# Two warming products, a fourth pair of banks for the first turns, modelled places for rectified differences, copies on VectorE, and a whole-row projection with single weighings in the last unit

## The chip, the cores and the metric

The kernel runs on one NeuronCore of one Trainium2 chip. The metric is the device time of one execution in microseconds. TensorE (PE, with its weight loads shown as PEld), VectorE (DVE), ScalarE (ACT), GpSimd (POOL) and SyncE (SP, which issues nearly all DMAs) run their own instruction streams in order and wait for each other by semaphores.

## The reference

One transformer block on a sequence of S = 2048 tokens of width D = 640: attention with H = 32 heads of 20, then a gated feed-forward of width F = 1728, both on layer-normed input and both added to it. All is float32.

```python
qkv = layernorm(x) @ wqkv                      # split into q, k, v and heads
scores = q @ k.T * Dh ** -0.5                  # per head
p = softmax(scores, axis=-1)
h = x + (p @ v) @ wo
z = layernorm(h)
h2 = h + (silu(z @ w_gate) * (z @ w_up)) @ w_down
```

## The kernel before

Products with full precision are made of three: each operand is split into a rounded high part and the rest (`split`: ACT copies, another engine subtracts), and hi·hi, hi·lo and lo·hi are summed in one PSUM bank. There are eight banks of 128 x 512.

**Beginning.** `load_x(0)` brings four tiles of 128 tokens. While they land, `warm` runs products that nothing reads (`ident` by the last of these tiles, L898), on a pair of banks from `ps_wide`. `norm(0)` normalises the tiles on DVE (L755); `flip_tokens` turns each by five TensorE transposes into a pair of banks (L801) and splits it from there into z_hi (ACT, L96) and z_lo (DVE, L97). `ps_wide` hands out its pairs of banks in rotation (`wide_places`). `first_blocks` then makes the first block of queries and the first block of keys (L826) in two banks with fixed numbers.

**Projection stage, to about 334 us.** A list `work` of blocks (`query_key`: 128 rows of queries or keys for 512 tokens) and values (`value`) runs in order. Their products (L569) use 64 rows of the array each, one half of the array beside the other. Between them stand turns of the next tokens (`flip`, L783), and products that find the maximum of each row of scores beforehand, as softmax needs it. These come in two kinds: pairs (L194), where the difference of two key blocks gives max(a, b) as relu(b − a) + a, with both parts of 256 columns in one bank; and opened products (L217), where a first product is rectified by ACT (L231) into a *place* in SBUF, and a second product, issued later on the same half, is added to it and maximised by DVE (L224). There are three such places, `relus`, taken in rotation by `next_place`. A key block or query block for these products is brought back from DRAM (`stack`, L161) into a free tile; tiles that are borrowed get the constant rows that they need by copying a piece of `w_hi` (`raw_place`, then `place`, L379, on ACT, four copies of 128 x 1024).

What order all this stands in is decided while the program is written, by a planner. The class `Halves` holds modelled clocks for the two halves, for each engine and for each bank; `use(engine, us)` advances one; `pair`, `finish_second`, `flip`, `run` and `keep` place the next instruction where these clocks say that nothing waits. The lengths in it (0.5 us for a copy of a block by ACT, for instance) are numbers in the code. On the chip the engines run this order with real semaphores: where a modelled length is too short, the engine waits, and all behind it on that engine. `self.second` holds the opened product of each half, at most one. `queries_at` says when the loaded queries of a unit are taken to have landed.

**Attention, units 0 to 31, to about 1476 us.** A unit is 4 heads by 512 queries. It has 16 steps over key tiles: four score products (`scores`, L1374, 62 rows, one half of the array each), their exponentials on ACT (L1380), and one `weigh` (L1384, four products of 32 columns on all 128 rows). `ORDER` is a string of the operations of a step; with no maxima left it is `sSsSW`. The letter W also runs one entry of `extra`: in the last unit (31) eight projections of the output by `wo` for chunk 1 (`projection`, L1103), three of layer norm, an empty one, and four turns (`flip`, L1135), one per step. With `halved` a projection is thirty products of 64 rows on the two halves, in two banks, added up by two DVE additions (L1109); without, it is fifteen of 128 rows in one bank. In the last unit `both` makes W run two weighings in each even step and none in odd ones.

**Feed-forward, to the end.** The same units of weights pass through rings of buffers; nothing here is touched.

Of the kernel before, what the change touches and what calls it, by code (L numbers as in the profile page):

```python
# [24 lines left out]
NT = S // P  # L25
# [15 lines left out]
MARGIN = 0.2  # L41
BEHIND = 2
# [7 lines left out]
def tile_block(ctx: ExitStack, tc: tile.TileContext, x, wqkv, wo, wg, wu, wd, out):  # L50
# [22 lines left out]
    wide_places, one_places = [2, 4, 6], []  # L73
# [264 lines left out]
    with tc.tile_pool(name="pa", bufs=2) as pa:  # L338
# [33 lines left out]
        def raw_place():  # L372
            return place(raw_tile().rearrange("p a b -> p (a b)")[:, : 2 * CH], nc.scalar)

        def place(t, engine=nc.sync):

            if engine is nc.scalar:
                some = w_hi.rearrange("p k c -> p (k c)")[:, : 2 * CH].bitcast(F32)
                nc.scalar.activation(t, some, AF.Copy)  # L379
# [64 lines left out]
        def staged_keys(u, kc, ks, q=None, since=0):  # L444
# [9 lines left out]
            def one(t, pair, b, at):  # L454
                rows = queries[u] if q is None else items[q][3]
                if b is None:
                    max_differences(mxs[u], rows, items[ks[0]][3], pair, t, kc, next_place(), at)
                    return over()
                first, more = (items[k][3] for k in ks)
                second = max_twice(mxs[u], rows, first, more, pair, t, kc, b, next_place(), at)  # L460
                return lambda at: (second(at), over())
# [15 lines left out]
            if u == 0:  # L477
# [5 lines left out]
                    lambda at, a=a: one(*a, at), a[2],  # L483
# [34 lines left out]
        def next_place():  # L518
            relus.append(relus.pop(0))
            return relus[-1]  # L520
# [9 lines left out]
        class Halves:  # L530
# [74 lines left out]
            def pair(self):  # L605
# [11 lines left out]
                if half is None and any(self.second) or half is not None and self.second[half]:  # L617
                    return False
# [3 lines left out]
                second = queue.pop(ahead)[1](at)  # L622
                if half is not None:
# [3 lines left out]
                    self.second[half] = second, seen  # L627
# [43 lines left out]
            def finish_second(self, half):  # L671
                if not self.second[half]:
                    return False
                second, seen = self.second[half]
# [3 lines left out]
                self.second[half] = None  # L678
                second(at)
                start = self.stream(half, 0.231)  # L680
                self.places[at[0]] = self.use("vector", 0.62, max(seen, start + 0.43)) + 0.14
                return True
# [136 lines left out]
        def first_blocks():  # L819

            z_hi, z_lo = zs[0]
            pss = ps_at(range(2))
# [7 lines left out]
            for m, ps in enumerate(pss):  # L830
                pe.places[m] = keep(0, m, ps)

        def keep(c, m, ps):
# [63 lines left out]
        for _ in range(3):  # L897
# [34 lines left out]
        for at, (kind, c, *which) in enumerate(work):  # L932
# [522 lines left out]
    for u in range(NU):  # L1455
# [4 lines left out]
        for kt in range(NT):  # L1460
# [5 lines left out]
            for op in order:  # L1466
# [4 lines left out]
                else:  # L1471
                    both = u == NU - 1 and kt < NT - 1
# [617 lines left out]
```

## Time and profile before

| | us |
|---|---|
| median of three runs (lowest, highest) | 2037.76 (2036.97, 2040.04) |
| the profiled execution, its own time | 2040.81 |
| its span, from first to last instruction | 2039.0 |
| granted TensorE clock, mean over the span | 0.996 |
| PE busy in the span | 2009.1 |
| ACT, DVE, POOL busy in the span | 1463.3, 1616.7, 778.5 |

Rows of a timeline read: start in us from the span's start, length in us, engine, line, operation, output and input tiles with shapes, count; in brackets the idle time of the engine before it and what ended it. The length of a row of several instructions is from the first start to the last end, and products overlap: from one to the next is shorter than one product's own length. `64*128` or `62*128` behind a product are the rows and columns of the array that it uses. Tiles have the names of the buffers that they borrow: queries and places appear as q_stk or v_stk, key blocks as k_stk or raw.

### The profile page before, as it was taken

Reading aid. Unit: us, or ns where it says so; the run is one execution under the profiler, and the core shown is the slowest. Engines: PE = TensorE matmul, PEld = TensorE weight load, DVE = VectorE, ACT = ScalarE, POOL = GpSimd, SP = SyncE. Lnnn points to the kernel's source line nnn. Section 1 sums busy time; section 2 is a strip of 40 time slices with the busy share of each in tenths; the row PEclk is TensorE's granted clock in tenths of the full one; section 3 lists DMA queues with packets and bytes.
Section 4 is the critical chain, followed back from the end, with each engine's and each line's share of the span. In section 5 each row is a group of like instructions: output and inputs, shape, how many; then the busy total and the mean of one; then the engine's idle time right before and its main releaser. Section 6 shows DMA issues by size and latency. Waiting matters only on the chain.

```text
span 2039.0 us, 39356 instructions
## 1 busy us (share of the span) xinstructions
PE 2009.1 (99%) x13836; PEld 1244.3 (61%) x13836; DVE 1616.7 (79%) x3261; ACT 1463.3 (72%) x2948; POOL 778.5 (38%) x1075
## 2 busy tenths in 40 slices
PE   7999999999999999999999999999999999999998
PEld 6888897333333333333333333345598888888888
DVE  7769776888888888888888888886478666676677
ACT  4887887999999999999999999996634222212221
POOL 4464342234343434344430011001146454754555
PEclk9999999999999999999999999999999999999999
DMA  7775574343533534444433123211159654974642
GB/s 228 236 214 184 167 215 116 104 137 103 150 125 108 158 112 143 135 145 137 149 127 108 30 61 83 82 62 49 36 180 325 208 193 154 350 267 158 204 149 92
DMA packets 205206, 304.93 MB, mean 150 GB/s; under 512 B 47648, under 2 KB 82720, under 8 KB 203984
## 3 DMA queue, kind: packets, MB, share of 16 engines
q1 hardware_dynamic: 204912, 302.40, 45.6%
q8 instruction: 110, 1.80, 0.4%
q14 instruction: 88, 0.72, 0.1%
q10 hardware_dynamic: 96, 0.00, 0.0%
HBM read 205.78 MB, written 95.68 MB: 148 GB/s over the span
## 4 chain that ended last, share of the span: by engine, by line
PE 94%; DMA 2%; DVE 1%; ACT 1%; POOL 1%; issue 1%; SPq 0%; DVEq 0%; ACTq 0%; POOLq 0%
PE banks L1384 25%; PE banks L1374 17%; PE banks L1552 16%; PE banks L238 12%; PE banks L1646 8%; PE banks L569 8%; PE banks L1103 3%; PE banks L217 3%; PE banks L194 1%; DMA qk_d<-e 0%; PE banks L826 0%; PE banks L263 0%; DMA q_stk<-qk_d 0%; ACT q_stk L231 0%; DMA xt<-in_A_x 0%
## 5 line engine op out<-in xcount | busy, mean ns | idle before, releaser
L1380 ACT ACTIVATE probs<-banks 128x512 f32<-128x512 f32 x2048 | 1056.2, 614 | 61.1 <-PE banks L1374 25.3
L244 DVE TENSOR_REDUCE mx<-banks 128x1 f32<-128x512 f32 x1472 | 925.4, 684 | 124.9 <-PE banks L238 76.3
L1374 PE MATMUL banks<-q_stk,k_stk 62*128 62x512 f32 x2048 | 583.2, 428 | 1.5 <-ACT probs L1380 1.5
L1384 PE MATMUL banks<-probs,v_stk 128*32 128x512 f32 x4096 | 545.4, 606 | 0.0
L238 PE MATMUL banks<-k_stk,q_stk 60*128 60x512 f32 x1472 | 486.7, 438 | 0.2
L1374 PEld LDWEIGHTS banks<-q_stk,k_stk 62*128 62x128 f32 x2048 | 291.8, 184 | 283.7 <-ACT probs L1380 271.4
L238 PEld LDWEIGHTS banks<-k_stk,q_stk 60*128 60x128 f32 x1472 | 244.2, 184 | 163.1 <-DVE mx L244 126.8
L1769 DVE TENSOR_TENSOR tmp<-banks,tmp 128x512 f32<-128x512 f32 x208 | 141.2, 689 | 118.4 <-PE banks L1552 92.8
L1384 PEld LDWEIGHTS banks<-probs,v_stk 128*32 128x32 f32 x4096 | 81.3, 108 | 183.1 <-issue 171.4
L1646 PE MATMUL banks<-halves,yp 128*128 128x320 f32 x1032 | 178.9, 308 | 1.4 <-POOL yp L97 1.2
L1646 PEld LDWEIGHTS banks<-halves,yp 128*128 128x128 f32 x1032 | 165.2, 188 | 17.4 <-POOL yp L97 1.5
L1552 PE MATMUL banks<-t,units 128*128 128x512 f32 x624 | 162.7, 396 | 0.1
L97 POOL TENSOR_TENSOR yp<-y,yp 128x256 fp32r<-128x256 f32 x96 | 60.3, 628 | 195.2 <-ACT yp L96 181.0
L1552 PE MATMUL banks<-z,units 128*128 128x512 f32 x516 | 133.8, 394 | 0.0
L255 POOL CAST both<-neg 128x16 fp32r<-128x16 f32 x32 | 6.6, 206 | 314.7 <-PE banks L1374 138.2
L1552 PEld LDWEIGHTS banks<-t,units 128*128 128x128 f32 x624 | 112.5, 188 | 18.9 <-DVE tmp L1769 0.3
L1651 DVE TENSOR_TENSOR h<-banks,h 128x320 f32<-128x320 f32 x248 | 110.0, 481 | 6.8 <-PE banks L1646 5.4
L224 DVE CUSTOM_DVE_ANT_0 q_stk<-banks,q_stk 128x512 f32<-128x512 f32 x139 | 92.7, 687 | 26.0 <-PE banks L217 13.2
L569 PE MATMUL banks<-z_hi,w_hi 64*128 64x512 f32 x380 | 102.4, 406 | 1.9 <-ACT z_hi L96 1.8
L569 PE MATMUL banks<-z_lo,w_hi 64*128 64x512 f32 x380 | 103.3, 395 | 0.0
L1552 PEld LDWEIGHTS banks<-z,units 128*128 128x128 f32 x516 | 93.1, 187 | 16.1 <-DVE tmp L1769 0.2
L96 ACT ACTIVATE yp<-tmp 128x512 fp32r<-128x512 f32 x40 | 25.3, 632 | 103.2 <-POOL tmp L1639 103.2
(213 smaller groups left out, 2960.9 us busy)
## 6 DMA issues: line engine op xcount, KB each, us to landing
units<-w_d SPq DMA_DIRECT2D x186, 256.0 KB
w_d<-stage SPq DMA_DIRECT2D x106, 256.0 KB
halves<-j_d SPq DMA_DIRECT2D x70, 320.0 KB
k_stk<-qk_d SPq DMA_DIRECT2D x116, 160.0 KB
j_d<-stage SPq DMA_DIRECT2D x42, 320.0 KB
q_stk<-qk_d SPq DMA_DIRECT2D x64, 160.0 KB
k_stk<-qk_d SPq DMA_DIRECT2D x116, 80.0 KB
rb<-r_d SPq DMA_DIRECT2D x32, 256.0 KB
```

Of the source, the lines that this page charges most:

```text
L217: nc.tensor.matmul(ps, q[rows, pair, t * P : (t + 1) * P], k[rows, pair, :], start=True, stop=True)
L224: nc.vector.tensor_tensor_reduce(out=place, in0=ps, in1=place, scale=1.0, scalar=LEAST, op0=ALU.add, op1=ALU.max, accum_out=mx[:, b, pair, ...
L238: nc.tensor.matmul(ps, queries[u][rows, pair, t * P : (t + 1) * P], keys[u // NC][rows, pair, kc * CH : (kc + 1) * CH], start=True, stop=True,
L244: nc.vector.tensor_reduce(mxs[u][:, b, pair, t, kc : kc + 1], ps, axis=AX.X, op=ALU.max)
L569: product = nc.tensor.matmul(job["ps"][:, :out], lhs, rhs, start=(half == 0 and i == 0), stop=(half == 1 and i == job["n"] - 1),)
L1374: nc.tensor.matmul(ps, keys[u // NC][rows, p, kt * P : (kt + 1) * P], queries[u][rows, p, :], start=True, stop=True,)
L1380: nc.scalar.activation(probs[p][:, b, :], ps, AF.Exp, scale=scale)
L1384: nc.tensor.matmul(acc[32 * j : 32 * j + 32, :], values[u // NC][:, kt, j * VW : j * VW + 32], probs[j // 2][:, j % 2, :], start=(kt == 0) ...
L1552: nc.tensor.matmul(ps.rearrange("p (t n) -> p t n", t=TPC), w[k][:, i], z[k][:, :, j], start=(first and m == 0), stop=(last and m == len(n ...
L1646: nc.tensor.matmul(ps, a, b, start=(n == 0), stop=(n == len(pairs) - 1))
L1651: nc.vector.tensor_tensor(out=h, in0=ps, in1=h, op=ALU.add)
L1769: add = lambda out, ps, x: nc.vector.tensor_tensor(out=out, in0=ps, in1=x, op=ALU.add)
```

## The change

It has six parts.

1. Two warming products instead of three.
2. `wide_places` has four pairs of banks, and `first_blocks` uses banks 2 and 3 instead of 0 and 1.
3. `raw_place` copies on DVE instead of ACT, and its modelled end counts before the tile is used.
4. The planner knows when each rectified place is free (`relu_at`); an operation on maxima starts only with a free place (`free_place`), the longest free one first. Each half may have two opened products (`OPEN`).
5. Modelled lengths: ACT's two copies of a block in `keep` 0.62 and 0.54 instead of 0.5 and 0.5; queries land 4.5 us after their modelled load instead of 3.5.
6. In the last unit the projection uses whole rows, and double weighings end at step 9 instead of step 14.

```diff
+OPEN = 2
-    wide_places, one_places = [2, 4, 6], []
+    wide_places, one_places = [0, 2, 4, 6], []
...
         def raw_place():
-            return place(raw_tile().rearrange("p a b -> p (a b)")[:, : 2 * CH], nc.scalar)
+            return place(raw_tile().rearrange("p a b -> p (a b)")[:, : 2 * CH], nc.vector)
...
-            if engine is nc.scalar:
+            if engine is nc.vector:
                 some = w_hi.rearrange("p k c -> p (k c)")[:, : 2 * CH].bitcast(F32)
-                nc.scalar.activation(t, some, AF.Copy)
-                pe.use("scalar", 1.0)
-                return t.rearrange("p (h n) -> p h n", h=2)
+                nc.vector.tensor_copy(t, some)
+                t = t.rearrange("p (h n) -> p h n", h=2)
+                place_at[id(t)] = pe.use("vector", 0.65) + 0.2
+                return t
...
-        def next_place():
-            relus.append(relus.pop(0))
-            return relus[-1]
+        relu_at = {}
+
+        def free_place(at):
+            place = min(relus, key=lambda r: relu_at.get(id(r), 0.0))
+            return place if relu_at.get(id(place), 0.0) <= at else None
...
-                self.second = [None, None]
+                self.second = [], []
...
-                if half is None and any(self.second) or half is not None and self.second[half]:
+                if half is None and any(self.second) or half is not None and len(self.second[half]) == OPEN:
                     return False
...
-                second = queue.pop(ahead)[1](at)
+                place = free_place(t + 0.43)
+                if place is None:
+                    return False
+                second = queue.pop(ahead)[1](at, place)
+                relu_at[id(place)] = math.inf
...
-                    self.second[half] = second, seen
+                    self.second[half].append((second, seen, place))
...
+                relu_at[id(place)] = self.places[at[1]]
...
-            pss = ps_at(range(2))
+            pss = ps_at((2, 3))
...
-                free = pe.use("scalar", 0.5, start)
-                done = pe.use("scalar", 0.5)
+                free = pe.use("scalar", 0.62, start)
+                done = pe.use("scalar", 0.54)
...
-        for _ in range(3):
+        for _ in range(2):
             nc.tensor.matmul(warm[:, 0], ident, xs[TPC - 1][:, :CH], start=True, stop=True)
...
-                    queries_at[u] = pe.sp(n=4, kb=750) + 3.5
+                    queries_at[u] = pe.sp(n=4, kb=750) + 4.5
...
-                    both = u == NU - 1 and kt < NT - 1
+                    both = u == NU - 1 and kt < NT // 2 + 2
...
-                        c - 1, ps_max if c < NC - 1 else (lambda: ps_b()), c == NC - 2
+                        c - 1, ps_max if c < NC - 1 else (lambda: ps_b())
```

The planner's new rules and lengths move instructions all through the projection stage. Three places matter below. The line numbers of the changed program are larger by 1 to 10.

On TensorE, behind the first turn of the projection stage (L783, in the changed program L793), before:

```order
L783 MATMUL banks<-ident,xt 128x64 x8
L569 MATMUL banks<-z_lo,w_hi 128x512
L194 MATMUL banks<-k_stk_116,q_stk 128x512 x2
L569 MATMUL banks<-z_hi,w_hi 128x512
L569 MATMUL banks<-z_lo,w_hi 128x512
```

and in the changed program, where L573 is the block product and L195 the pair:

```order
L793 MATMUL banks<-ident,xt 128x64 x8
L573 MATMUL banks<-z_lo,w_hi 128x512
L573 MATMUL banks<-z_hi,w_hi 128x512
L573 MATMUL banks<-z_lo,w_hi 128x512
L573 MATMUL banks<-z_hi,w_hi 128x512
L573 MATMUL banks<-z_lo,w_hi 128x512
L573 MATMUL banks<-z_hi,w_hi 128x512
L573 MATMUL banks<-z_lo,w_hi 128x512
L573 MATMUL banks<-z_hi,w_hi 128x512
L573 MATMUL banks<-z_lo,w_hi 128x512
L195 MATMUL banks<-k_stk_116,q_stk 128x512 x2
```

The first pair on the queries of unit 0 stands behind nine block products instead of one.

On ACT, a little later, before (L205 rectifies pairs, L351 and L96 copy a block, L791 a turn):

```order
L205 ACTIVATE q_stk<-banks 128x256 x4
L351 ACTIVATE v_stk_117<-banks 128x512
L96 ACTIVATE v_stk_117<-v_stk_117 128x512
L791 ACTIVATE xt<-banks 128x4x64 x2
L96 ACTIVATE z_hi<-xt 128x512
L379 ACTIVATE raw<-w_hi 128x1024 x3
L205 ACTIVATE v_stk_117<-banks 128x256 x2
```

and DVE in the changed program there (L208 is the maximum of a pair, L98 the second part of a block):

```order
L208 ISA v_stk_117,mx_121<-banks,v_stk_117 128x256
L208 ISA mx_121 128x1
L380 CAST raw<-w_hi 128x1024 x3
L98 TENSOR_TENSOR v_stk_117<-v_stk_117 128x512
L208 ISA q_stk,mx_121<-banks,q_stk 128x256
```

The three copies have left ACT's queue, where a pair's rectified halves stood behind them, and stand on DVE between two groups of pairs.

On TensorE in the last unit, from the last projection on, before (L1103 projection, L1374 scores, L1384 weighings, four products each, L1135 turns):

```order
L1103 MATMUL banks<-wo_hi,o_lo 128x320 x8
L1374 MATMUL banks<-q_stk,k_stk_4721 128x512 x4
L1384 MATMUL banks<-probs,v_stk_4722 32x512 x8
L1374 MATMUL banks<-q_stk,k_stk_4721 128x512 x8
L1384 MATMUL banks<-probs,v_stk_4722 32x512 x8
L1374 MATMUL banks<-q_stk,k_stk_4721 128x512 x8
L1384 MATMUL banks<-probs,v_stk_4722 32x512 x8
L1135 MATMUL banks<-ident,z_17209 128x128 x5
L1374 MATMUL banks<-q_stk,k_stk_4721 128x512 x4
```

and in the changed program (L1113, L1384, L1394 and L1145 in the same roles):

```order
L1113 MATMUL banks<-wo_hi,o_lo 128x320 x5
L1384 MATMUL banks<-q_stk,k_stk_4720 128x512 x4
L1394 MATMUL banks<-probs,v_stk_4721 32x512 x8
L1384 MATMUL banks<-q_stk,k_stk_4720 128x512 x8
L1394 MATMUL banks<-probs,v_stk_4721 32x512 x4
L1384 MATMUL banks<-q_stk,k_stk_4720 128x512 x4
L1394 MATMUL banks<-probs,v_stk_4721 32x512 x4
L1384 MATMUL banks<-q_stk,k_stk_4720 128x512 x4
L1394 MATMUL banks<-probs,v_stk_4721 32x512 x4
L1145 MATMUL banks<-ident,z_17076 128x128 x5
```

Scores of two steps ahead of two weighings became scores of one step ahead of one weighing from step 10 on.

More of the change, by code (lines that the diff above doesn't have):

```diff
@@ L452, in staged_keys, with one @@
                 all_products = [(t, pair, None) for t in range(TPC) for pair in range(2)]
-            def one(t, pair, b, at):
+            def one(t, pair, b, at, place):
                 rows = queries[u] if q is None else items[q][3]
                 if b is None:
-                    max_differences(mxs[u], rows, items[ks[0]][3], pair, t, kc, next_place(), at)
+                    max_differences(mxs[u], rows, items[ks[0]][3], pair, t, kc, place, at)
                     return over()
                 first, more = (items[k][3] for k in ks)
-                second = max_twice(mxs[u], rows, first, more, pair, t, kc, b, next_place(), at)
+                second = max_twice(mxs[u], rows, first, more, pair, t, kc, b, place, at)
                 return lambda at: (second(at), over())
@@ L482, in staged_keys @@
                     and (q is not None or pe.now() >= queries_at.get(u, math.inf)),
-                    lambda at, a=a: one(*a, at), a[2],
+                    lambda at, place, a=a: one(*a, at, place), a[2],
                 )
@@ L673, in finish_second @@
                     return False
-                second, seen = self.second[half]
+                second, seen, place = self.second[half][0]
                 at = self.banks(1)
@@ L677, in finish_second @@
                     return False
-                self.second[half] = None
+                del self.second[half][0]
                 second(at)
@@ L681, in finish_second @@
                 self.places[at[0]] = self.use("vector", 0.62, max(seen, start + 0.43)) + 0.14
+                relu_at[id(place)] = self.places[at[0]]
                 return True
@@ L830, in first_blocks @@
             for m, ps in enumerate(pss):
-                pe.places[m] = keep(0, m, ps)
+                pe.places[2 + m] = keep(0, m, ps)
         def keep(c, m, ps):
```

## The prediction

> **What bounds the kernel now.** I read the page's chain of waits first, then the stretches by stage (length, then busy time of PE, PEld, DVE, ACT and POOL, the granted clock, the DMA share and GB/s), then what TensorE waited for up to 335 us (total, times, longest).
>
> ```profile
> PE 94%; DMA 2%; DVE 1%; ACT 1%; POOL 1%; issue 1%; SPq 0%; DVEq 0%; ACTq 0%; POOLq 0%
> ```
>
> ```profile
> 24.00:334.00 310.00, 298.34 (x2791) 278.17 (x2792) 230.59 (x828) 244.10 (x533) 141.00 (x117) 0.98 0.65 201
> ...
> 1420.00:1476.00 56.00, 54.95 (x475) 32.42 (x474) 25.03 (x62) 38.77 (x77) 7.51 (x5) 0.97 0.12 33
> ```
>
> ```profile
> PE banks L217 <- ACT q_stk L231: 4.3, 5, 1.6
> ...
> PE banks L194 <- DMA q_stk<-qk_d: 1.3, 2, 1.0
> PE banks L217 <- ACT v_stk L231: 1.2, 1, 1.2
> ```
>
> 94% of the chain is TensorE's own work. So only three places can give: the start before 24 us, the projection stage (24 to 334 us; 310 − 298.3 = 11.7 us idle), and the last unit. The change touches these three and nothing between. Units 0 to 30 and the feed-forward half keep their instructions, and what is saved ahead of them passes through.
>
> A long idle costs twice, since the clock drops (the same view, PE alone):
>
> ```profile
> 46.94:50.35 3.41, 3.41 (x18) 0.50 0.59 179
> ...
> 60.59:64.00 3.41, 3.37 (x23) 0.50 0.59 210
> ...
> 173.23:176.64 3.41, 3.41 (x20) 0.50 0.31 118
> ...
> 1463.47:1466.88 3.41, 3.41 (x20) 0.50 0.02 5
> ```
>
> Each of these is 3.41 us at half clock, 1.7 us of work lost, and each comes just behind a stall.
>
> **The start.**
>
> ```profile
> 7.68 5.36 PE L898 MATMUL banks<-xt,ident 128*128 128x512 f32 x6 [7.68 <-DMA xt<-in_A_x]
> ...
> 11.07 1.66 DVE L755 TENSOR_SCALAR xt<-xt,mv,r_a 128x640 f32<-128x640 f32 x3
> ...
> 12.88 1.80 PE L801 MATMUL banks<-ident,xt 128*128 128x128 f32 x15
> ...
> 13.62 1.90 ACT L96 ACTIVATE z_hi<-banks 128x640 fp32r<-128x640 f32 x3 [2.86 <-PE banks L801]
> ...
> 15.24 0.77 PE L801 MATMUL banks<-ident,xt 128*128 128x128 f32 x5 [0.56 <-DVE z_lo L97]
> 16.05 0.70 ACT L96 ACTIVATE z_hi<-banks 128x640 fp32r<-128x640 f32 x1 [0.53 <-PE banks L801]
> ...
> 16.80 2.58 PE L826 MATMUL banks<-z_hi,w_hi 128*128 128x512 f32 x10 [0.79 <-ACT z_hi L96]
> ```
>
> ```profile
> L801 PEld LDWEIGHTS banks<-ident,xt x20: 139/141/231, 12.1 to 15.6; 128*128 128x128 f32 x20
> ```
>
> The three warming products are six passes of about 0.86 us. The first normalised tile is there at 11.07 + 0.55 = 11.6, but the first turn waits for the sixth pass, to 12.88. With two products PE is free at 7.68 + 4 × 0.86 = 11.1, so the turn starts about 11.8. The longest weight load, 231 ns, is the one at 12.1, against a median of 141: the clock was still low there, so this turn is slow and ends near 13.0, about 0.6 earlier. The fourth turn waited for the first pair of banks (DVE z_lo, 0.56, after more idle). With a fourth pair it follows at once, and the four copies at 0.63 run through: 13.05 + 4 × 0.63 = 15.6 against 16.75. So the first blocks start 1.1 us earlier. They move to banks 2 and 3, which the first turn has long left. **Term: −1.1**, between −1.2 and +0.3 (below).
>
> **The projection stage.** The order of the two programs shows the pairs' first products eight block products later (the queries' modelled landing is 1 us later), and three copies of rows moved from ACT to DVE.
>
> ```profile
> 46.00 0.47 PE L194 MATMUL banks<-k_stk,q_stk 60*128 60x512 f32 x1 [1.03 <-DMA q_stk<-qk_d]
> 46.79 0.63 PE L194 MATMUL banks<-k_stk,q_stk 60*128 60x512 f32 x1 [0.32 <-DMA q_stk<-qk_d]
> ```
>
> A whole product of 512 columns takes 0.26 (L826, ten in 2.58), and two products on the two halves run side by side in that, so eight more cover 1.0 of this 1.03 + 0.32. If that keeps the clock, another 1.7 comes back: at most −3.1, at least 0 if the queries land later too. I take **−2.0**.
>
> ```profile
> 56.56 2.93 ACT L379 ACTIVATE raw<-w_hi 128x1024 fp32r<-128x1024 f32 x3
> ...
> 59.79 0.42 DVE L207 CUSTOM_DVE_ANT_0 v_stk<-banks,v_stk 128x256 f32<-128x256 f32 x1 [5.30 <-ACT v_stk L205]
> ...
> 60.28 0.93 PE L783 MATMUL banks<-ident,xt 64*128 64x64 f32 x7 [1.65 <-DVE mx L207]
> ```
>
> (The views are the timelines of ACT, DVE and PE.) Three copies hold ACT for 2.93 us. Behind them stand a pair's rectified halves, then DVE's maxima (idle 5.30 us), then the banks that the next turn needs: PE stalls 1.65 us and the clock falls. On DVE a copy of 1,024 columns is bounded by scaling 0.55 us for 640 columns (0.9) and ACT's 1.04. Three take some 3 us of DVE's idle 5.3, with twelve block products and a turn between these pairs and the next. Without that cover the maxima would be late by those 3 us, and the stall would stand. At most −1.65 − 1.7 = −3.35; taken **−3.0**; at worst 0.
>
> The rest is the rectified places.
>
> ```profile
> L231 ACT ACTIVATE q_stk<-banks 128x512 f32<-128x512 f32 x139 | 80.1, 595 | 18.1 <-DVE mx L224 7.0 <-PE banks L217 5.0 <-PE banks L569 4.6
> ```
>
> ```profile
> 168.87 1.21 DVE L106 TENSOR_SCALAR r_a<-v_a 128x4 int32<-128x4 int32 x1
> ...
> 171.35 0.16 DVE L106 TENSOR_TENSOR t_a<-t_a,r_a 128x4 f32<-128x4 f32 x1
> ```
>
> ```profile
> 168.76 2.53 POOL L431 TENSOR_TENSOR k_stk<-k_stk,raw 128x512 fp32r<-128x512 f32 x2
> ```
>
> ACT stood 7.0 us because a place was not yet emptied by DVE; PE's share of this is the 4.3 + 1.2 = 5.5 us of L217 waits and one half-clock stretch, 7.2 together. The new rule starts no product without a free place, and counts ACT's own copies nearer to their length. But DVE was late for a reason the plan does not know: an operation of 0.16 us took 1.21 beside POOL's differences. Two open products per half also change every later position. Nothing here shows that the new order meets POOL less. From −7.2 (all gone) to +7.2 (doubled) I take **−0.5**, near zero since its cause stays.
>
> [...]
>
> **The last unit.**
>
> ```profile
> 1380.27 1.00 PE L1103 MATMUL banks<-wo_hi,o_hi 128*128 128x320 f32 x5
> ...
> 1382.67 0.49 PE L1374 MATMUL banks<-q_stk,k_stk 62*128 62x512 f32 x1
> ```
>
> ```profile
> 1431.65 1.00 PE L1103 MATMUL banks<-wo_hi,o_hi 64*128 64x320 f32 x10
> ...
> 1433.96 0.63 PE L1374 MATMUL banks<-q_stk,k_stk 62*128 62x512 f32 x4
> 1434.43 0.98 PE L1103 MATMUL banks<-wo_hi,o_hi 64*128 64x320 f32 x8
> ```
>
> ```profile
> 1453.08 1.92 PE L1384 MATMUL banks<-probs,v_stk 128*32 128x512 f32 x16
> ...
> 1472.06 0.77 PE L1135 MATMUL banks<-ident,z 128*128 128x128 f32 x5
> 1472.75 0.73 PE L1374 MATMUL banks<-q_stk,k_stk 62*128 62x512 f32 x4
> 1473.41 1.06 PE L1384 MATMUL banks<-probs,v_stk 128*32 128x512 f32 x8
> 1474.41 0.77 PE L1135 MATMUL banks<-ident,z 128*128 128x128 f32 x5
> ...
> 1476.38 1.00 PE L1103 MATMUL banks<-wo_hi,o_hi 128*128 128x320 f32 x5
> ```
>
> ```profile
> 1455.47 4.03 ACT L1380 ACTIVATE probs<-banks 128x512 f32<-128x512 f32 x8 [0.64 <-PE banks L1374]
> ```
>
> Whole rows alone cost time. A projection of fifteen whole products lasts 1382.67 − 1380.27 = 2.40, of thirty halves 2.31; four scores ahead of a half product last 0.47, ahead of a whole one 0.66. So a step without weighing loses 0.28 and one with weighing 0.1 or nothing: over eight steps +0.9 to +1.4, taken +0.9. The eight DVE additions saved are not waited for.
>
> The single weighings gain it back. From step 8's weighing to the end the unit took 1476.38 − 1453.08 = 23.3 us. Eight scores ran ahead of two weighings, so ACT starved, and PE starved in turn to half clock. In the new order each step's scores come before one weighing: 1.85 for step 8's pair, three steps at ACT's 4.03 / 2 = 2.0, four steps of 0.66 + 1.00 + 0.69 = 2.35 (scores, weighing, turn), and 1.9 for the last two weighings: 19.2. That is −4.1, and −3.2 with the whole rows. If the clock falls once more, 1.7 of it goes. **Term: −2.3**, between −3.2 and +0.9 (nothing gained).
>
> **Sum:** −1.1 − 2.0 − 3.0 − 0.5 − 2.3 = −8.9. The profiled execution's own 2040.81 (span 2039.0, 1.8 around it) becomes 2031.9. It lies 3.1 above the median of the three runs, 2037.76, from which the same sum gives **2028.9**.
>
> **Rivals.**
> 1. The new order gives the stage's gain back: it removes two stalls and makes others, since DVE beside POOL is not in its model. For it: 7.0 us of ACT's waits have that cause. Against: the two large stalls have causes that the order does remove. Then −1.1 − 2.3 is left and some 0.5: 2034.
> 2. Slower: two open products a half put off DVE's maxima, and each time three places are full ACT's queue stands, with the copies of blocks and turns behind it. Six L217 waits cost 7.2 us, 1.2 each. At 7 more the gain of 8.9 is gone; at twelve more, 14 us, the time is 2043.
> [...]
> 4. The last unit gains nothing, because its turns wait for DVE: +0.9 instead of −2.3, 2032.1.
>
> **Chances.** Forecast 0.57 (own range 2024 to 2033.5), rival 1 0.16, rival 2 0.09, rival 3 0.10, rival 4 0.08. A measurement of this kernel tells 0.2%, 4.1 us, from no change: faster is below 2033.7, slower above 2041.8. Faster: 0.53 + 0.06 + 0.09 + 0.05 = 0.73. Slower: 0.08 of rival 2. Same: 0.19. The range leaves out rival 2 and a tenth below: 2022.5 to 2037.5, by bounds of −15 and 0.
>
> **What would show it.** The first L826 near 15.7. No 1.65 us wait of a turn near 57 us, and no half-clock stretch before 100 us. ACT's wait for DVE's maxima below 7.0. The stage ending near 328 instead of 334. From step 8's weighing to the next projection about 19 to 21 us. It is wrong if new L217 waits of a microsecond and more appear in number.

## The result, and the profile after

| | before | after |
|---|---|---|
| median (lowest, highest) | 2038.62 (2036.97, 2040.04) | 2028.34 (2026.63, 2029.93) |
| span of the profiled execution | 2039.0 | 2028.1 |
| first warming product to first block product | 9.12 | 7.57 |
| first block product to first score product of unit 0 | 317.55 | 308.83 |
| units 0 to 30 | 1087.63 | 1087.75 |
| last unit: first of eight projections to step 8's weighing | 29.20 | 30.08 |
| step 8's weighing to the next projection | 23.30 | 20.70 |
| from there to the end | 562.65 | 563.38 |

The ratio is 0.9952, 95% interval 0.9938 to 0.9965: 9.8 us faster, with 2028.9 forecast. Nearly all of it lies ahead of attention: in the profiles the first score product comes 10.1 us earlier, at 324.27 instead of 334.35. The chain of waits still ends on TensorE throughout:

```profile
PE 94%; DMA 2%; DVE 2%; ACT 1%; POOL 1%; issue 1%; SPq 0%; ACTq 0%; DVEq 0%; POOLq 0%
```

The stretches of the projection stage and of the last unit, after (length, then busy time of PE, PEld, DVE, ACT and POOL, granted clock, DMA share, GB/s):

```profile
24.00:324.00 300.00, 293.76 (x2787) 272.47 (x2786) 232.92 (x827) 239.59 (x527) 139.49 (x117) 1.00 0.66 207
1410.00:1466.00 56.00, 55.55 (x364) 31.02 (x363) 22.40 (x56) 39.47 (x78) 7.55 (x5) 0.97 0.11 33
```

The same products now take 300 us instead of 310. PE idles 6.2 us instead of 11.7, and the clock is 1.00 instead of 0.98: none of the stage's three half-clock stretches is left in this execution (3 × 1.7 = 5.1 us of work). What PE waits for there, after (total, times, longest):

```profile
PE banks L573 <- ACT z_hi L97: 2.0, 2, 1.1
PE banks L573 <- DVE mx L225: 1.2, 1, 1.2
PE banks L218 <- POOL z_lo L433: 1.1, 2, 0.7
PE banks L793 <- DVE mx L208: 0.7, 1, 0.7
...
PE banks L218 <- ACT q_stk L232: 0.2, 1, 0.2
```

L218 is the opened product, L217 before: its waits for ACT fell from 4.3 + 1.2 to 0.2. The waits for loaded queries are gone in this profile. The turn of next tokens (L793) waits 0.7 where it waited 1.65. A second profile of the same stage, that of the kernel with the last unit as before (below), has a wait of 0.5 for queries and one half-clock stretch, at 83.7 us (its clock from 24 to 325 us is 0.99).

ACT's rectifications of opened products (busy, mean ns, then the idle time ahead of them and what ended it), before with places in v_stk (the prediction has the row for q_stk), then both rows after:

```profile
L231 ACT ACTIVATE v_stk<-banks 128x512 f32<-128x512 f32 x69 | 41.1, 596 | 4.8 <-PE banks L217 2.3 <-DVE mx L224 2.0
```

```profile
L232 ACT ACTIVATE q_stk<-banks 128x512 f32<-128x512 f32 x140 | 81.7, 597 | 9.7 <-PE banks L218 3.9 <-DVE mx L225 2.6 <-PE banks L573 1.7
L232 ACT ACTIVATE v_stk<-banks 128x512 f32<-128x512 f32 x68 | 40.5, 596 | 9.0 <-PE banks L218 5.0 <-DVE mx L225 2.7 <-PE banks L573 0.8
```

For places that DVE had not yet emptied, ACT waited 7.0 + 2.0 us before and waits 2.6 + 2.7 after.

The start of the timeline, after:

```profile
7.87 3.75 PE L908 MATMUL banks<-xt,ident 128*128 128x512 f32 x4 [7.87 <-DMA xt<-in_A_x]
11.78 2.72 PE L811 MATMUL banks<-ident,xt 128*128 128x128 f32 x20 [0.15 <-DVE xt L765]
15.44 2.58 PE L836 MATMUL banks<-z_hi,w_hi 128*128 128x512 f32 x10 [0.94 <-ACT z_hi L97]
```

All twenty transposes stand in one row: the fourth turn no longer waits for a pair of banks.

The last unit from step 8 on, after (timeline of PE, then one stretch of 3.41 us as above):

```profile
1444.02 1.92 PE L1394 MATMUL banks<-probs,v_stk 128*32 128x512 f32 x16
1445.87 0.74 PE L1384 MATMUL banks<-q_stk,k_stk 62*128 62x512 f32 x4
1447.06 1.97 PE L1384 MATMUL banks<-q_stk,k_stk 62*128 62x512 f32 x4 [0.45 <-ACT probs L1390]
1448.96 1.48 PE L1394 MATMUL banks<-probs,v_stk 128*32 128x512 f32 x8
1450.37 1.22 PE L1384 MATMUL banks<-q_stk,k_stk 62*128 62x512 f32 x4
```

```profile
1449.48:1452.89 3.41, 3.41 (x20) 0.70 (x12) 0.00 (x0) 2.65 (x6) 0.00 (x0) 0.50 0.00 0
```

Step 8 still weighs twice and step 9 not at all, so eight scores run in a row, PE waits 0.45 us for ACT, and 3.41 us at a clock of 0.50 follow.

### The profile page after: what moved, and what is told of

Read it like the earlier page. It is cut to its first block, busy times and chain, and to the rows that moved or that the text cites. A ratio compares the mean times of both kernels' runs of the same rounds, so it can differ in the third digit from the quotient of the medians.

```text
span 2028.1 us, 39119 instructions
## 1 busy us (share of the span) xinstructions
PE 2003.9 (99%) x13714; PEld 1236.9 (61%) x13714; DVE 1617.4 (80%) x3257; ACT 1460.4 (72%) x2944; POOL 778.9 (38%) x1075
## 3 DMA queue, kind: packets, MB, share of 16 engines
q8 instruction: 109, 1.79, 0.4%
## 4 chain that ended last, share of the span: by engine, by line
PE 94%; DMA 2%; DVE 2%; ACT 1%; POOL 1%; issue 1%; SPq 0%; ACTq 0%; DVEq 0%; POOLq 0%
PE banks L1394 25%; PE banks L1384 17%; PE banks L1562 16%; PE banks L239 12%; PE banks L1656 8%; PE banks L573 8%; PE banks L1113 3%; PE banks L218 3%; PE banks L195 1%; DMA halves<-j_d 0%; DMA units<-w_d 0%; PE banks L836 0%; PE banks L264 0%; DMA xt<-in_A_x 0%; PE banks L1145 0%
## 5 line engine op out<-in xcount | busy, mean ns | idle before, releaser
L1384 PE MATMUL banks<-q_stk,k_stk 62*128 62x512 f32 x2048 | 581.5, 430 | 1.1 <-ACT probs L1390 1.1
L1394 PE MATMUL banks<-probs,v_stk 128*32 128x512 f32 x4096 | 545.4, 605 | 0.0
L1384 PEld LDWEIGHTS banks<-q_stk,k_stk 62*128 62x128 f32 x2048 | 290.3, 185 | 285.3 <-ACT probs L1390 271.3
L1394 PEld LDWEIGHTS banks<-probs,v_stk 128*32 128x32 f32 x4096 | 81.0, 108 | 182.6 <-issue 170.6
L98 POOL TENSOR_TENSOR yp<-y,yp 128x256 fp32r<-128x256 f32 x96 | 60.5, 630 | 195.0 <-ACT yp L97 180.9
L573 PE MATMUL banks<-z_hi,w_hi 64*128 64x512 f32 x380 | 105.2, 395 | 2.2 <-ACT z_hi L97 2.0
L573 PE MATMUL banks<-z_lo,w_hi 64*128 64x512 f32 x380 | 105.3, 393 | 0.0
L573 PE MATMUL banks<-z_hi,w_lo 64*128 64x512 f32 x380 | 101.9, 391 | 0.0
```

What stands on the lines that cost most here:

```text
L573: product = nc.tensor.matmul(job["ps"][:, :out], lhs, rhs, start=(half == 0 and i == 0), stop=(half == 1 and i == job["n"] - 1),)
L1384: nc.tensor.matmul(ps, keys[u // NC][rows, p, kt * P : (kt + 1) * P], queries[u][rows, p, :], start=True, stop=True,)
L1394: nc.tensor.matmul(acc[32 * j : 32 * j + 32, :], values[u // NC][:, kt, j * VW : j * VW + 32], probs[j // 2][:, j % 2, :], start=(kt == 0) ...
```

## The experiments

Twelve kernels, each with 4 to 12 executions, and each compared with executions of the kernel before in its own round; the median of before moves by 0.7 us between rounds. The mean clock is that of the timed executions: it differs between executions of one program, and matters below. "Stage" is the time from the first block product to the first score product in the one profiled execution.

| kernel | median | ratio to before, 95% | mean clock | stage |
|---|---|---|---|---|
| before | 2038.1 to 2038.8 | 1 | 0.9977 | 317.55 |
| the change | 2028.34 | 0.9952 (0.9938 to 0.9965) | 0.9990 | 308.83 |
| before + start | 2036.78 | 0.9994 (0.9985 to 1.0004) | 0.9975 | 313.83 |
| before + copies | 2042.63 | 1.0021 (1.0011 to 1.0031) | 0.9980 | 319.19 |
| before + queries' landing | 2042.91 | 1.0018 (1.0009 to 1.0027) | 0.9975 | 317.99 |
| change without modelled places | 2034.37 | 0.9981 (0.9971 to 0.9991) | 0.9990 | 313.68 |
| change, one open product a half | 2030.40 | 0.9966 (0.9953 to 0.9979) | 0.9966 | 307.19 |
| before + modelled places | 2028.17 | 0.9951 (0.9939 to 0.9963) | 0.9988 | 309.25 |
| change, last unit as before | 2031.86 | 0.9970 (0.9958 to 0.9982) | 0.9984 | 310.66 |
| change, halves, single from step 8 | 2027.57 | 0.9957 (0.9940 to 0.9974) | 0.9990 | 308.34 |
| change, choice of place only | 2032.61 | 0.9972 (0.9963 to 0.9981) | 0.9988 | 311.12 |
| change, refusal only | 2031.40 | 0.9964 (0.9952 to 0.9977) | 0.9963 | 309.64 |
| before + places, start, new last unit | 2024.98 | 0.9936 (0.9923 to 0.9948) | 0.9987 | 306.61 |
| the same + copies | 2022.70 | 0.9924 (0.9910 to 0.9938) | 0.9990 | 302.34 |

### The start alone

```diff
-    wide_places, one_places = [2, 4, 6], []
+    wide_places, one_places = [0, 2, 4, 6], []
...
-            pss = ps_at(range(2))
+            pss = ps_at((2, 3))
...
-        for _ in range(3):
+        for _ in range(2):
             nc.tensor.matmul(warm[:, 0], ident, ...)
```

> The kernel before with the two edits of the start alone (two warming products, a fourth pair of banks, first blocks in banks 2 and 3); every other instruction keeps its place. Theory of the start: the first blocks begin at 15.4 to 15.7 us instead of 16.8, and the first score product at 332.9 to 333.3 instead of 334.35, since the stage is a chain of TensorE's own work: 1.1 to 1.4 us of the whole. Rival: the first queries land by a DMA chain of their own, so the later stalls grow and the first score product stays at 334.0 to 334.4. [...]

1.6 us faster by medians, 1.2 by the ratio, not told apart from none. In the profile the blocks start 1.6 us earlier (15.20) and the first score 5.3 (329.03), earlier than either expectation: the wait for queries shrank to 0.5 and its half-clock stretch did not come, though the queries' landing was untouched. Part of this was lost again behind the stage: attention began at half clock (0.51 from 332.8 to 336.3 us), and unit 0 took 36.20 us instead of 34.56.

### The copies alone on VectorE

```diff
-                nc.scalar.activation(t, some, AF.Copy)
-                pe.use("scalar", 1.0)
...
+                nc.vector.tensor_copy(t, some)
...
+                place_at[id(t)] = pe.use("vector", 0.65) + 0.2
```

> The kernel before with the four copies of borrowed tiles on DVE alone. Theory of named waits: the 1.65 us wait of a turn near 58.6 us and the half-clock stretch at 60.6 go, the one at 46.9 stays; the first score product comes 2.6 to 3.4 us earlier, 331.0 to 331.8. Rival, re-planning: the order behind the copies changes too, and gives back up to 3 us in other waits, so that the first score product stays within 333.5 to 335.

Slower by 4.3 us. The stage's stretch and two rows of its timeline of PE:

```profile
24.00:335.00 311.00, 301.31 (x2789) 275.93 (x2788) 236.44 (x830) 240.16 (x529) 140.78 (x118) 1.00 0.65 200
```

```profile
159.35 0.50 PE L217 MATMUL banks<-raw,q_stk 60*128 60x512 f32 x1 [1.38 <-ACT q_stk L231]
...
170.30 0.50 PE L217 MATMUL banks<-raw 60*128 60x512 f32 x1 [1.44 <-ACT q_stk L231]
```

The named stall and all half clock in the stage are gone, as intended (1.00). But the first score product stands at 335.73, 1.4 us later than before and beyond both expectations. The planner made another order from there on. In it opened products wait 5.1 us for ACT, nearly as long as before (5.5). PE idles 2 us less than before and yet is busy 301.3 us at full clock with the products that took 298.3 at 0.98; why they take longer in this order, no run shows. Unit 0 then takes 36.18 us, as long as with the start alone (36.20), where attention began at 0.51.

### The queries' later landing alone

```diff
-                    queries_at[u] = pe.sp(n=4, kb=750) + 3.5
+                    queries_at[u] = pe.sp(n=4, kb=750) + 4.5
```

> The kernel before with the later modelled landing of the queries alone. Theory of named waits: the waits of 1.03 and 0.32 us for the queries near 46 us and the half-clock stretch at 46.9 go, 2.0 to 3.1 us; the copies are still on ACT, and unless the later pairs happen to miss them, the stretch at 60.6 stays. First score product 331.3 to 332.4. Rival, re-planning: within 1 us of 334.35.

Slower by 4.5 us by medians, 3.7 by the ratio. Both waits for queries went, and opened products now wait 5.9 us for ACT in the profile. The first score product stands at 334.43, as the rival expected. The profiled execution was the fastest of the ten (2039.55), so the rest of the loss is in no profile.

### Everything but the modelled places

```diff
-                place = free_place(t + 0.43)
-                if place is None:
-                    return False
-                second = queue.pop(ahead)[1](at, place)
+                second = queue.pop(ahead)[1](at)
```

with `next_place` and one opened product per half as before.

> The changed kernel with the rectified places as before: three in rotation, not modelled, one opened product per half; the start, the copies, the queries, the lengths and the last unit as changed. Theory of named waits: the two stalls before 65 us stay away, and only the waits behind places not yet emptied come back, up to 7.2 us of L217 and half clock; I took 0.5 for this part, so the first score product at 324.8 (324.3 in the changed kernel), and ACT waits for DVE's maxima as long as in the changed kernel, 5.3 us. Rival, places: those waits were really removed by the modelled places; then ACT's wait for DVE's maxima is 8 to 9 us as in the kernel before (9.0), L217 waits of 3 to 5 us return, and the first score product is at 327.5 to 329.

Only 0.9981: 6 us of the 9.8 go with this one part. The first score product stands at 328.80, and ACT waits 8.6 us for DVE's maxima, both as the rival said. The waits that the part removes are back:

```profile
PE banks L217 <- ACT v_stk L231: 2.3, 2, 1.3
PE banks L217 <- ACT q_stk L231: 2.2, 3, 1.1
```

### One opened product per half

```diff
-OPEN = 2
+OPEN = 1
```

> The changed kernel with at most one opened product per half (as before the change); the modelled places, free_place and all the rest kept. If knowing when a place is free is what saves, the first score product stands near 324.3 as in the changed kernel (within 1.5) and the time is within 2 us of 2028.3. If having two opened products per half is what saves, the first score stands near 328.8, as with the places taken in rotation, and the time near 2034. ACT's wait for DVE's maxima (lines of L231/L232): at or below 5.3 by the first, near 8.6 by the second.

The stage is the shorter one (307.2, PE idle 3.9 us; ACT waits 4.5 us for DVE's maxima), so the gain is not due to two opened products. The runs are 2 us behind the change with overlapping intervals, and the mean clock is 0.9966 instead of 0.9990. Three stretches in a row, from 319.25 to 329.49 us, around the first score product at 322.70, are at half clock in its profile; this is the first:

```profile
319.25:322.66 3.41, 3.18 (x11) 2.56 (x9) 3.41 (x21) 3.25 (x11) 0.00 (x0) 0.51 0.24 65
```

### The modelled places alone

Part 4 of the change on the kernel before, with two opened products per half and nothing else.

> The kernel before with the modelled places and two opened products per half alone: no change to the start, copies, queries' landing, block lengths or the last unit. If this part pays by itself (the 4.5 us that it was worth inside the change), the first score product stands near 330 instead of 334.4 and the time near 2034, with the L217 waits of 5.5 us in all down to 2. If it pays only together with the others (the wait for the queries and the 1.65 us turn stay, and the order behind them moves again), the first score stands at 333 or later and the time is 2037 or more.

2028.17: as much as the whole change, and better than either expectation. PE's waits in the stage:

```profile
PE banks L572 <- ACT z_hi L97: 1.7, 2, 1.1
PE banks L572 <- DVE mx L208: 1.7, 1, 1.7
PE banks L792 <- DVE mx L208: 1.7, 1, 1.7
PE banks L195 <- DMA q_stk<-qk_d: 0.7, 1, 0.7
...
PE banks L218 <- ACT q_stk L232: 0.2, 1, 0.2
```

The 5.5 us of opened products are 0.2. The stage is 8.3 us shorter than before, about what 5.3 us of these waits and two half-clock stretches fewer (3.4 us) make. One of the two had followed the wait for queries, which is still there (0.7), so it need not have gone with the places. The turn behind the copies still waits its 1.7, and behind it lies the only half-clock stretch of this execution's stage (0.51 from 58.68 to 62.09 us).

### The last unit as before

```diff
-                    both = u == NU - 1 and kt < NT // 2 + 2
+                    both = u == NU - 1 and kt < NT - 1
...
-                        c - 1, ps_max if c < NC - 1 else (lambda: ps_b())
+                        c - 1, ps_max if c < NC - 1 else (lambda: ps_b()), c == NC - 2
```

> The changed kernel with the last unit as it was before (projections on halves, double weighings up to step 14). Everything ahead of the last unit is the same. By the profiles: the first eight projections 29.2 us instead of 30.1, step 8's weighing to the next projection 23.3 instead of 20.7; so 1.7 us slower than the changed kernel, 2030.0. If the last unit were worth the 2.3 of the prediction, 2030.6; if nothing, 2028.3.

3.5 us slower than the change in the runs, with overlapping intervals. The projections took 29.21, the part from step 8 on 21.66, without a half-clock stretch there this time; before, with one (0.50 from 1463.47 us), 23.30. Where both or neither have the stretch, the change's last unit is 1.1 to 1.7 us shorter (before's 29.20 + 23.30 against 30.08 + 20.70; 29.21 + 21.66 here against 30.12 + 19.68 in the choice-only kernel below, which had none). Between this profile and the change's, nearly the whole difference lies ahead of the last unit, where the two are one program: this one has half-clock stretches at 83.7 and 329.5 us that the other has not.

### Halves kept, single weighings from step 8

```diff
-                    both = u == NU - 1 and kt < NT // 2 + 2
+                    both = u == NU - 1 and kt < NT // 2
```

and `halved` kept, as above.

> The changed kernel with the projection of the last unit on halves as before the change, and single weighings from step 8 on instead of step 10. If whole rows cost 0.9 and the eight scores in a row before step 8's weighing starve ACT and bring the half-clock stretch, the first eight projections take 29.2 us instead of 30.1, step 8's weighing to the next projection about 19 instead of 20.7 with no half-clock stretch, and the time is 2026 (2.5 less than the changed kernel). If the half clock comes from something else in that unit (the turns' waits, say), only the 0.9 comes back: 2027.4.

The profile shows what was expected: 29.21 and 18.92 us, no half clock (mean clock of the profiled execution 1.0).

```profile
1443.06 1.06 PE L1394 MATMUL banks<-probs,v_stk 128*32 128x512 f32 x8
1444.06 1.29 PE L1384 MATMUL banks<-q_stk,k_stk 62*128 62x512 f32 x4
1445.28 1.07 PE L1394 MATMUL banks<-probs,v_stk 128*32 128x512 f32 x8
...
1460.13 1.92 PE L1394 MATMUL banks<-probs,v_stk 128*32 128x512 f32 x16
1461.98 0.41 PE L1113 MATMUL banks<-wo_hi,o_hi 128*128 128x320 f32 x1
```

Scores and weighings alternate without a wait. In the runs this is 0.8 us by medians, within the intervals; one of its six executions took 2038.33.

### Which half of the place rule

The first kernel chooses the place that is modelled free first and never refuses; the second keeps the rotation and refuses. Both have one opened product per half.

```diff
-            return place if relu_at.get(id(place), 0.0) <= at else None
+            return place
```

```diff
-            place = min(relus, key=lambda r: relu_at.get(id(r), 0.0))
-            return place if relu_at.get(id(place), 0.0) <= at else None
+            if relu_at.get(id(relus[0]), 0.0) > at:
+                return None
+            relus.append(relus.pop(0))
+            return relus[-1]
```

> The changed kernel with one opened product per half, and free_place that takes the place that is modelled free first but never refuses. TensorE's order, POOL's and SP's are those of the kernel with places in rotation (2034.37, first score 328.80); only which of the three places 35 of ACT's rectifications and their maxima use is another. If the choice of the place is what saves, the L218 waits of 4.5 us fall below 2, the first score stands near 324 to 325 and the time near 2030. If starting no product without a free place is what saves, nothing changes: first score 328.8, time 2034.

> The changed kernel with one opened product per half, places in rotation as before the change, but no product started while the next place in the rotation is modelled as taken. If the refusal is what saves, this is as good as with the free choice (a_open1: first score 322.7, 2030.4): first score 322 to 325, time 2029 to 2031. If the choice is needed too, the first score stands at 326 to 329 and the time at 2032 to 2034.

The choice left 3.3 us of L218 waits for ACT of the 4.5, and 2032.61: at most 1.8 us gained, between the two expectations. With the refusal alone no wait of L218 for ACT is listed any more, and PE idles 4.65 us before attention, close to the 3.85 with both halves of the rule; 2031.40 against 2030.40. The intervals of the two kernels overlap, so it is the waits that say that the refusal carries it; the first score at 325.04 and the time are at the edge of what was expected.

### The parts that paid, together

Modelled places, the start, halves in the last unit and single weighings from step 8; then the copies as well.

> The parts that paid alone, together: modelled places with two opened products per half, the start (two warming products, four pairs, banks 2 and 3), and the last unit with projections on halves and single weighings from step 8; copies stay on ACT, the queries' landing and the block lengths as before. From the kernel before with the places alone (2028.17): the start 1.1 less, the last unit 50.9 - 48.1 = 2.7 less: 2024.4, faster than the changed kernel by 3.9. If the start brings nothing beside the places, as the stage's other edits do not, 2025.5; if the new order behind the start loses what it saves, 2027.6, as the changed kernel with that last unit.

> As the one before, with the three copies on VectorE too (so the changed kernel without the queries' landing and block lengths, with the better last unit). If copies on VectorE save the turn's stall of 1.66 us near 56 us and its half-clock stretch of 1.7 beside modelled places, 2021; if, as in the kernel before, the new order gives it back elsewhere, 2024 to 2027.

Both beat the kernel before. The first is where it was expected; the second, between its two expectations, beats the change by 5.6 us, with intervals that only touch. It differs from the kernel with halves and single weighings from step 8 (2027.57) in two things alone: the queries' landing (3.5) and the lengths of ACT's block copies (0.5, 0.5) are as before. Those two edits cost 4.9 us by medians of different rounds, with intervals that just miss each other. The waits of PE, first with them, then without:

```profile
PE banks L573 <- ACT z_hi L97: 2.1, 2, 1.2
PE banks L573 <- DVE mx L225: 1.2, 1, 1.2
PE banks L218 <- DVE mx L225: 0.9, 1, 0.9
PE banks L793 <- DVE mx L208: 0.7, 1, 0.7
```

```profile
PE banks L195 <- ACT v_stk L206: 0.7, 1, 0.7
PE banks L1384 <- ACT probs L1390: 0.6, 1, 0.6
PE banks L573 <- DMA raw<-qk_d: 0.6, 1, 0.6
PE banks L573 <- ACT z_hi L97: 0.5, 2, 0.2
PE banks L195 <- DMA q_stk<-qk_d: 0.5, 1, 0.5
```

PE's idle time from 24 us to the first score fell from 6.2 to 2.7. The wait for queries is 0.5 without any later landing.

## Why the prediction was right, and where its parts were wrong

The total came out for other reasons than the sum gave, and that it lies within 1 us of the forecast is luck: the places, taken at 0.5 us, brought some 10, and the later landing, which was to bring 2.0, cost time together with the longer block copies. In medians the parts stack up like this, in one order of adding them: places −10.2 (2038.4, the middle of the medians of before, to 2028.17), start and a better last unit −3.2 (2024.98), copies −2.3 (2022.70), landing and lengths +4.9 (2027.57), and the change's own last unit in place of the better one +0.8 (2028.34). The first step and the +4.9 are outside the intervals of their neighbours, the others are not.

**The start, −1.1: right in the profiles.** The turns start at 11.78 (11.8 forecast), and the fourth no longer waits for banks; what each of the two edits is worth alone was not tried. That the clock was still low in the first turn is read from its weight loads: 231 ns at 12.1 before, where loads of this shape (L1135) had a median of 225 in the stretch at 0.50 from 1463.47 us and of 140 in the whole trace; the clock column itself shows 1.00 there. Over all profiles with three warming products the first block comes 8.65 us after the first warming product (four, 8.21 to 9.12), with two 7.47 (ten, 7.25 to 8.22): −1.2. Rival 3, a start that stays slow for longer, showed in part in one profile of the ten (turns of 3.42 us, in the others 2.40 to 2.72; first block after 8.22). The bound of +0.3 is shown by no run: in all ten the first block comes earlier than the 9.12 of before.

**The queries' stall, −2.0: wrong.** The stall did go in the change's profile, and its half-clock stretch. But the edit alone cost 4.5 us, and the stall also shrank to 0.5 with the start alone and in the fastest kernel, and went with the copies alone, all with the earlier landing. The later landing was credited with what other edits brought as well. Beside the places it and the lengths together cost 4.9; which of the two was not tried there. The cost of the landing alone makes it the likelier.

**The copies, −3.0: right only beside modelled places.** The three take 2.99 us on DVE, with some 3 worked out, but by luck: two took 0.69 each and the third, beside a subtraction on POOL, 1.79, where 0.9 to 1.04 was taken for each. The turn waits 0.73:

```profile
49.44 2.99 DVE L380 CAST raw<-w_hi 128x1024 fp32r<-128x1024 f32 x3
```

Beside the places that is −2.3, within the intervals; alone it was +4.3. That is rival 1 in kind: the new order gave the gain back, and more.

**The places, −0.5: the mis-sized step.** They are worth 10 us alone and 6 on top of the rest; the prediction counted 7.2 us for all of these waits together, and kept 0.5. The failed sentence is that DVE "was late for a reason the plan does not know" and that the term stays "near zero since its cause stays". Such slow operations did stay. Operations of DVE that took over 0.25 us longer than the median of their kind (line, operation and shape), while POOL worked, number ten in the stage before, twelve in the change and 13 with the places alone. Two of the change's, and POOL's operations beside the first:

```profile
160.17 1.23 DVE L107 TENSOR_TENSOR t_a<-t_a,r_a 128x4 f32<-128x4 f32 x1
...
163.15 0.74 DVE L107 SCALAR_TENSOR_TENSOR r_a<-t_a,r_a 128x4 f32<-128x4 f32 x1
```

```profile
160.07 2.56 POOL L433 TENSOR_TENSOR raw<-raw,k_stk 128x512 fp32r<-128x512 f32 x2 [4.93 <-DMA raw<-qk_d]
```

The median of either kind is 0.16 (and that of the first of the prediction's two rows, which are of different kinds, 0.17, where it took 1.21). The waits of opened products for ACT fell from 5.5 to 0.2 us nevertheless.

The plan of before broke its own clocks: counted in the planner, 89 of its 288 operations on maxima were started while the place that was next in rotation was still taken by its model, by up to 3.0 us of its own clocks; in 88 of the 89 no other place was free either, which fits that refusing helped and choosing gained little. ACT then stood with all behind it. On the chip it stood eight times for a place, 9.0 us in all, and seven of these waits, 8.2 us, are at products that the plan had started in this way. The slow operations on DVE may have lengthened some of them. The order already held this, and the prediction looked for the cause in slow operations around 168.9 us instead. Rival 2, harm from two opened products, is not shown: the profiled stage is 1.6 us shorter with one, and the runs are 2 us slower, within the intervals.

**The last unit, −2.3: mechanism right, size a little less.** Whole rows cost 0.88, with 0.9 taken, though four steps at the 0.28 worked out make 1.1. The weighings gave 2.6, net −1.7. The term held some chance of another half-clock stretch, and it came (0.50 from 1449.48 us): behind the double weighing of step 8, which the working passed over as one pair of 1.85 us. Without it the change's order takes 19.68 (choice-only kernel), with 19.2 worked out. With single weighings from step 8 on (18.92) the steps last 2.0 to 2.2 and, with a turn, 2.35 to 2.4 us, close to the 2.0 and 2.35 worked out. Rival 4 falls.

**What would show it:** the first block product (L826, now L836) at 15.44 (15.7 forecast), no wait of 1.65 near 57 us, no half clock before 100 us, ACT's waits for DVE's maxima 5.3 us, all as said, but the second profile of this stage has the half-clock stretch at 83.7 us. The 7.0 that the prediction set as a bound for ACT's waits was one of two rows; together they were 9.0. The stage ended at 324.3 instead of 328; that is the places' share showing.

## What to carry to other kernels

Where a planner hands out a buffer, let it refuse while the buffer is taken by its own clocks: count such violations in the plan before looking for causes on the chip. An edit that removes a named stall from an order that is planned greedily changes everything behind it, so it is judged alone and beside the others: two stall removals here cost over 4 us each alone, and the later landing, with the longer block copies, cost 4.9 inside the change as well. A right total does not show right parts.

## What was not expected of the hardware

The granted clock differed between two profiled executions of the same program, by stretches of 3.41 us. Up to the last unit the change and the kernel with the last unit as before are one program. In the profile of the one the start of attention ran at 1.00, in that of the other at 0.50:

```profile
328.41:331.82 3.41, 3.41 (x29) 1.48 (x22) 2.19 (x5) 3.33 (x8) 3.36 (x2) 1.00 0.53 148
```

```profile
329.50:332.90 3.40, 3.40 (x15) 1.18 (x11) 1.32 (x3) 1.99 (x5) 3.35 (x2) 0.50 0.49 143
```

15 products instead of 29, and unit 0 takes 36.15 us instead of 34.57. Over 58 executions of the kernel before, the median is 2036.98 at a mean clock of 0.999 and 2039.99 at 0.996. In the last unit the double weighings up to step 14 met such a stretch in three of six profiles, the change's order in four of five, the alternating one in none of three. Differences of 2 us are therefore read from several executions, or from rows at full clock.

The prediction put each half-clock stretch down to a stall just ahead of it. But waits as long were not always followed by one: of those before that last 1.0 us and more, the ones that ended at 46.0, 60.3 and 172.9 us (1.03, 1.65 and 1.62 us) were, the ones that ended at 220.4, 233.7 and 272.1 us (1.19, 1.01 and 1.19 us) were not: a long idle cost twice in three cases of six. And TensorE was not idle for long ahead of the stretch in the last unit: it shows as busy for 2.96 of 3.41 us. The clock fell 23 times between 20 and 1480 us in the 14 profiles, and each time TensorE had started only 8 to 18 products in the 3.41 us ahead. With this part of each profile counted off in lengths of 3.41 us, the clock fell after 23 of the 93 lengths with 18 products or fewer, and after none of the 5841 with more.

The two kernels that refuse and have one opened product per half show a lower mean clock (0.9966 and 0.9963 against 0.9990), with less idle time: in their profiles three stretches follow one another around the start of attention, 10.2 us in all (0.51 in the first of the one and from 322.8 to 326.2 us in the other), behind 3.41 us with 10 and 9 products started. Whether the one opened product brings this was not tried.
